# The first batch's transpose: through HBM, or by six copies within SBUF from column-tiled products

## The chip, the cores and the metric

The kernel runs on one core of a Trainium2 chip. The metric is device time in microseconds for one launch; a run of the kernel before takes 618.25 us (median of three). Engines are named as in the profile: PE (TensorE), DVE (VectorE), ACT (ScalarE), POOL (GpSimd) and SP, whose queue issues most of the DMAs.

## The reference, cut to what matters

```python
# x: (8, 3008, 256); w_gate, w_val: (256, 1536); w_out: (1536, 256)
X = np.fft.fft(x, axis=1)          # over the 3008 positions of each batch
X = np.fft.fft(X, axis=2)          # over the 256 channels
y = X.real.reshape(8 * 3008, 256)
g = y @ w_gate
gelu = 0.5 * g * (1 + erf(g / sqrt(2)))
out = (gelu * (y @ w_val)) @ w_out
```

The real part of a two-dimensional Fourier transform is followed by a gated feed-forward block.

## The kernel before, in words

The transform over 3008 = 64 x 47 positions is done in two stages of matmuls. The transform over the channels is folded into the weights: `gen_w` multiplies the cast weights `wb` by a cosine and sine table `CW` and makes three bf16 weight tiles, `WE` (even part), `WOP` (odd part) and `WOM`, which is `WOP` times `col_m` (0 for the first channel, -2 for the others): added to a sum that already holds the `WOP` product, it turns the sign of the odd part.

For each batch:

- `load_x` brings three pieces of x into `xins`; `fold_x` forms sums and differences of channel c and 256 - c into `xf` (batch 0 on DVE, later batches on POOL); `singles` copies the two channels that have no partner.
- Stage one, `a_step(b, k)`: for two of the 24 slots `jj`, one matmul each with weights `G[:, jj, :]` (128 x 128, a table made on the chip by `phase_g`, `sin_g`, `turn_g`) and 256 moving columns `xf[jj]`. The products are copied from PSUM to the tile `S1`.
- The turn: `z_write` stores `S1` to a scratch tensor `z` in HBM, and `z_read` loads it back into `Ap` with other rows on the partitions. In batch 0 there are six writes of four slots each, and after all of them six reads: three thirds, each in two halves of 16 of the 32 groups. Each third lands on every fourth partition of `Ap`; the partitions that no third reaches stay at the zeros that two POOL memsets put there.
- Stage two, `b_steps(b, eo, q)`: for each of 32 groups, a matmul of `Ap` with a table of 47 or 48 columns (`TP`, `TQ`, or `T0P`, `T0Q` for group 0), for the even and the odd part; for batch 0 another 32 with a single weight column. `evac_rest` and `evac_top` copy the results into `Y`.
- The feed-forward block runs in 36 units per batch (three column chunks of `Y` times twelve slices of 128 features): value and gate matmuls with `WE`, `WOP`, `WOM`, Gelu on ACT, products on DVE and POOL into `h`, then the second layer with `Wo_sb`.

The order on each engine is the program's order: the wrapper `_InOrder` keeps every instruction where it is written. Before the first unit the program issues, in this order, tables for stage one, folds, stage one and z writes of batch 0, a few warming matmuls (`warm`), the z reads, loads of the next weights and of batch 1, the tables `CW` and `TP`, `TQ`, `T0P`, `T0Q`, the first quarter `gen_w(0, ...)` of the weights, and stage two of batch 0 in two halves: groups 0 to 15 of the even and the odd part need only the first half of the z reads, groups 16 to 31 need the second. Units 0 to 7 of batch 0 also generate the other weights (`extra`), and from unit 4 on batch 1's stages are woven in.

`CW` has two halves for the 256 channels, each with its phase tile (`phase_c`), its reduction (`reduce_c`) and its sine (`sin_c`).

Of the kernel before, what the change touches and what calls it, by code (L numbers as in the profile page):

```python
# [37 lines left out]
def kernel(  # L38
# [27 lines left out]
    NJ = 48  # L66
# [46 lines left out]
    col_c = [const_pool.tile([128, 1], FP32, name=f"col_c{i}") for i in range(2)]  # L113
# [7 lines left out]
    rowt = work.tile([128, 4 * N2 + 2 * NJ + 2 * NG], FP32, tag="osb", bufs=2, name="rowt")  # L121
    quat = work.tile([128, 4 * N2 + 2 * NJ + 2 * NG], FP32, tag="osb", bufs=2, name="quat")
# [139 lines left out]
    def quats():  # L262
        for o, b0 in ((0, 0.25), (2 * N2, 0.0)):
            vec.tensor_scalar(
                _sub(quat, [[1, 2 * N2]], o), _sub(cols, [[0, 2 * N2]], 1),
                0.25, b0, op0=ALU.mult, op1=ALU.add)

    TO = 4 * N2
    iota(_sub(rowt, [[2 * N2, 2], [1, 2 * N2]], 0), [[0, 2], [1, 2 * N2]], 0, 0)
# [88 lines left out]
    def sin_t(ph, red):  # L358
        s = lambda t, o, n: _sub(t, [[1, n]], o)
        act.activation(TP[:, :], s(red, 0, 2 * N2), AF.Sin, scale=col_w)  # L360
        act.activation(TQ[:, :], s(red, 2 * N2, 2 * N2), AF.Sin, scale=col_w)
        act.activation(s(ph, 0, 2 * NJ), s(red, 4 * N2, 2 * NJ), AF.Sin, scale=col_w)
        act.activation(_sub(TB, [[1, 2 * NG]], 0), s(red, TG, 2 * NG), AF.Sin, scale=col_w)
        for i, t in enumerate((T0P, T0Q)):
            vec.tensor_scalar(
                t[:, :MID], s(ph, i * NJ, MID), cols[:, 3:4], None, op0=ALU.mult)
            vec.tensor_scalar(
# [4 lines left out]
    def cols_c():  # L372
        for t in range(NCH):
            pool.tensor_scalar(col_c[t], col_p, 128.0 * t, 1.0 / C, op0=ALU.add, op1=ALU.mult)

    def phase_c(t):
        both = red2_tile()
        redc.append(both)
        for q, (o, n) in enumerate(((0, 129), (129, 127))):
            pool.tensor_scalar(both[:, o : o + n], rowc[:, o : o + n], col_c[t], 0.25 * (q + 1),  # L380
                               op0=ALU.mult, op1=ALU.add)

    def reduce_c():
        for both in redc:
            reduce_phase(both[:, :C], both[:, C : 2 * C])
        vec.tensor_scalar(col_m, col_p, 1.0, -2.0, op0=ALU.is_ge, op1=ALU.mult)

    def sin_c():
        for t in range(NCH):
            act.activation(  # L390
                _sub(CW, [[1, C]], t * C), redc[t][:, C : 2 * C], AF.Sin, scale=-TWO_PI)
# [13 lines left out]
    def gen_w(f0, i, eo, bank, o=0, n=512):  # L405
# [7 lines left out]
        if eo == 0:  # L413
            on_half(ps, act.activation(WE[:, i, fs], out, AF.Copy))
        else:
            on_half(ps, act.activation(WOP[:, i, fs], out, AF.Copy))
            on_half(ps, vec.tensor_scalar(
                WOM[:, i, fs], out, col_m, None, op0=ALU.mult))
# [627 lines left out]
```

## Time and profile before

| | |
|---|---|
| runs | 618.25 us median of 3 (618.23 to 620.0) |
| profiled execution | 617.78 us, its span 616.0 us |
| PE busy | 600.3 us (97% of the span) |
| DVE busy | 568.8 us (92%) |
| ACT busy | 487.9 us (79%) |
| POOL busy | 503.8 us (82%) |
| first stage-one matmul | 9.1 us from the span's start |
| first matmul of unit 0 | 26.98 us |

Times in the profile count from the first instruction of the span; the rest of the execution's time lies around the span. Busy time is an average over stages with different limits. Matmuls overlap in the records, so the distance between starts says more than the duration of one. The chain of waits goes back from the last instruction to what released each step. The granted TensorE clock reads full in all stretches.

### The profile page before, as it was taken

The page shows a single profiled execution, that of the slowest core. Times are in us where ns is not written, and L with a number is a line of the kernel's source. Part 1 is how long each engine was busy: PE and PEld are TensorE (multiplying, and loading weights), DVE is VectorE, ACT ScalarE, POOL GpSimd, SP SyncE. Part 2 cuts the span into 40 slices and gives each one's busy share as a digit, 9 for nine tenths or more (in the row PEclk, how much of TensorE's full clock was granted, in tenths as well). Part 3 has the DMA queues.
Part 4 walks back from the last instruction along what each step waited for, and adds up shares of the span by engine and source line. Part 5 has one row for each costly group of instructions (what it writes and reads, how often), then busy time and mean ns, then how long its engine had stood idle before and what let it go on. Part 6 is the DMA issues. An engine that isn't in the chain of part 4 may idle for free.

```text
span 616.0 us, 12987 instructions
## 1 busy us (share of the span) xinstructions
PE 600.3 (97%) x4554; PEld 398.7 (65%) x4554; DVE 568.8 (92%) x690; ACT 487.9 (79%) x1009; POOL 503.8 (82%) x521
## 2 busy tenths in 40 slices
PE   3899999999999999999999999999999999999997
PEld 2456666666676666666666666666666666666666
DVE  8688999999999999999999999999999999999992
ACT  8788878977898778877789778887788878767762
POOL 9297999889999899798998899898997755665552
PEclk9999999999999999999999999999999999999999
DMA  8997423662236612663146532375123611211113
GB/s 323 338 296 252 147 61 117 176 199 91 76 121 206 201 44 77 189 227 113 52 131 174 196 95 77 105 222 197 57 67 97 193 49 45 61 50 53 37 51 86
DMA packets 65474, 82.35 MB, mean 134 GB/s; under 512 B 8218, under 2 KB 58906, under 8 KB 62498
## 3 DMA queue, kind: packets, MB, share of 16 engines
q1 hardware_dynamic: 63698, 80.62, 41.7%
q0 software_dynamic: 1552, 0.79, 0.9%
q8 instruction: 35, 0.57, 0.4%
q14 instruction: 29, 0.24, 0.1%
q10 hardware_dynamic: 160, 0.13, 0.1%
HBM read 45.05 MB, written 37.25 MB: 134 GB/s over the span
## 4 chain that ended last, share of the span: by engine, by line
PE 92%; DVE 3%; ACT 2%; DMA 1%; SPq 1%; issue 0%; ACTq 0%; DVEq 0%
PE ps_o L25 38%; PE ps_g L25 28%; PE ps_v L25 20%; PE ps_d L25 6%; DVE xf L25 1%; DMA Ap<-z 1%; DVE dv L25 1%; ACT glp L25 1%; SPq L25 1%; DVE ev L25 0%; DVE h L25 0%; ACT glm L25 0%; ACT S L25 0%; DMA out_dram<-osb 0%; ACT WE L25 0%
## 5 line engine op out<-in xcount | busy, mean ns | idle before, releaser
L25 POOL TENSOR_TENSOR h<-glm,dv 128x1024 bf16<-128x1024 bf16 (+1 forms) x138 | 291.2, 2112 | 82.2 <-DVE dv L25 62.2
L25 PE MATMUL ps_o<-Wo_sb,h 128*128 128x256 bf16 x2124 | 284.2, 272 | 0.0
L25 PEld LDWEIGHTS <-h 128*128 128x128 bf16 x2208 | 211.0, 98 | 58.3 <-issue 0.9
L25 DVE SCALAR_TENSOR_TENSOR ev<-nq,WN,ps_v 128x512 f32<-128x512 bf16 (+1 forms) x276 | 202.1, 733 | 23.0 <-PE ps_v L25 14.7
L25 ACT ACTIVATE glp<-ps_g 128x512 bf16<-128x512 f32 (+1 forms) x288 | 169.9, 590 | 37.0 <-PE ps_g L25 25.3
L25 ACT ACTIVATE glm<-ps_g 128x512 bf16<-128x512 f32 (+1 forms) x241 | 142.2, 590 | 57.4 <-PE ps_g L25 44.5
L25 DVE TENSOR_TENSOR h<-glp,ps_v 128x1024 bf16<-128x1024 bf16 (+2 forms) x150 | 172.9, 1153 | 5.4 <-ACT glp L25 3.7
L25 DVE SCALAR_TENSOR_TENSOR dv<-ev,ps_v 128x1024 f32<-128x1024 f32 (+1 forms) x138 | 164.8, 1194 | 0.0
L25 POOL TENSOR_TENSOR xf<-xin 128x254 bf16<-128x254 f32 x168 | 118.5, 728 | 0.8 <-PE ps_g L25 0.8
L25 PE MATMUL ps_v<-Y,WE 128*128 128x512 bf16 (+1 forms) x288 | 108.0, 375 | 0.0
L25 PE MATMUL ps_v<-Y,WOP 128*128 128x512 bf16 (+1 forms) x288 | 107.7, 374 | 0.1
L25 PE MATMUL ps_g<-Y,WOP 128*128 128x512 bf16 (+1 forms) x288 | 107.6, 374 | 0.0
L25 PE MATMUL ps_g<-Y,WE 128*128 128x512 bf16 (+1 forms) x288 | 107.6, 374 | 0.0
L25 PE MATMUL ps_g<-Y,WOM 128*128 128x512 bf16 (+1 forms) x241 | 90.3, 375 | 0.1
L25 PEld LDWEIGHTS <-WOP 128*128 128x128 bf16 x576 | 55.5, 97 | 49.3 <-ACT WOP L25 0.4
L25 PEld LDWEIGHTS <-WE 128*128 128x128 bf16 x576 | 56.0, 97 | 27.5 <-issue 2.0
L25 ACT ACTIVATE osb<-ps_o 128x512 f32<-128x512 f32 x92 | 54.2, 589 | 13.4 <-PE ps_o L25 12.6
L25 POOL TENSOR_TENSOR go<-go,ge 128x480 f32<-128x480 f32 (+1 forms) x47 | 58.2, 1238 | 7.0 <-DVE go L25 6.5
L25 PEld LDWEIGHTS <-Ap 128*128 128x128 bf16 (+1 forms) x561 | 39.6, 95 | 33.2 <-issue 1.4
L25 ACT ACTIVATE S<-ps_d 128x512 bf16<-128x512 f32 x82 | 48.9, 596 | 0.2 <-PE ps_d L25 0.2
L25 PEld LDWEIGHTS <-G 128*128 128x128 bf16 x213 | 21.8, 103 | 32.5 <-issue 11.0
L25 DVE SCALAR_TENSOR_TENSOR go<-nq,WN,ps_g 128x480 f32<-128x480 bf16 (+1 forms) x47 | 34.3, 729 | 2.6 <-ACT glp L25 1.9
(132 smaller groups left out, 377.1 us busy)
## 6 DMA issues: line engine op xcount, KB each, us to landing
out_dram<-osb SPq DMA_DIRECT2D x358, 64.0 KB
xin<-in_x_dram SPq DMA_DIRECT2D x16, 1024.0 KB
Ap<-z SPq DMA_DIRECT2D x21, 512.0 KB
xin<-in_x_dram SPq DMA_DIRECT2D x8, 896.0 KB
z<-S SPq DMA_DIRECT2D x7, 768.0 KB
z<-S SPq DMA_DIRECT2D x7, 512.0 KB
z<-S SPq DMA_DIRECT2D x13, 256.0 KB
nq<-nrow SPq DMA_DIRECT2D x8, 376.2 KB
```

The costliest lines, as they stand in the source:

```text
L25: return lambda *a, **k: self._tc.keep_in_program_order(call(*a, **k))
```

## The change

Six things are changed, all of them before or around the first units of batch 0.

1. Stage one of batch 0 is done by `a_group(J)`, J = 0 to 5, each for four slots `jj`. For every slot there are four matmuls with 32 of the 128 weight columns each; the outputs of the four slots go to four different ranges of 32 partitions of one PSUM tile. The twelve evacuations are all on ACT.
2. One DMA per group copies `S1` (128 partitions of 2 KB) directly to 16 partitions of `Ap` (every fourth, from `J % 2 * 64 + J // 2`), 16 KB into each. The z writes and z reads of batch 0 are gone. Every group of stage two now reads data of all six copies.
3. `CW`'s second half is formed on ACT from the first by copies with signs +1 and -1, instead of by a phase and sine of its own; the remaining phase is made on ACT, not POOL.
4. The tables `TP` and `TQ` take half as many phases (each is written twice from the same phases); `quats` and the products for `T0P` and `T0Q` move from DVE to POOL; `cols_t` moves ahead of the second fold; the third fold is done in two halves.
5. `WOM` is formed on DVE from `WOP` in SBUF (`turn_w`), not from PSUM; for the first quarter of the weights this comes after unit 0's first-layer matmuls. The first `WE` quarter is evacuated by DVE, not ACT.
6. Order: the tables and the Gelu table load come before `gen_w(0, ...)`; the warming matmuls are 6, not 5 and 16; stage two runs all even groups, then all odd ones, then the single columns, and then the evacuations.

```diff
     def quats():
-        for o, b0 in ((0, 0.25), (2 * N2, 0.0)):
-            vec.tensor_scalar(
+        for o, b0 in ((0, 0.25), (N2, 0.0)):
+            pool.tensor_scalar(
...
     def sin_t(ph, red):
-        act.activation(TP[:, :], s(red, 0, 2 * N2), AF.Sin, scale=col_w)
-        act.activation(TQ[:, :], s(red, 2 * N2, 2 * N2), AF.Sin, scale=col_w)
-        act.activation(s(ph, 0, 2 * NJ), s(red, 4 * N2, 2 * NJ), AF.Sin, scale=col_w)
+        act.activation(s(ph, 0, 2 * NJ), s(red, TO, 2 * NJ), AF.Sin, scale=col_w)
+        for i, t in enumerate((TP, TQ)):
+            act.activation(
+                _sub(t, [[N2, 2], [1, N2]], 0), _sub(red, [[0, 2], [1, N2]], i * N2), AF.Sin, scale=col_w)
...
     def sin_c():
-        for t in range(NCH):
-            act.activation(
-                _sub(CW, [[1, C]], t * C), redc[t][:, C : 2 * C], AF.Sin, scale=-TWO_PI)
+        act.activation(_sub(CW, [[1, C]], 0), redc[0][:, C : 2 * C], AF.Sin, scale=-TWO_PI)
+        for o, sign in ((0, 1.0), (1, -1.0)):
+            act.activation(_sub(CW, [[2, 128]], C + o), _sub(CW, [[2, 128]], o), AF.Copy, scale=sign)
...
         if eo == 0:
-            on_half(ps, act.activation(WE[:, i, fs], out, AF.Copy))
+            on_half(ps, act.activation(WE[:, i, fs], out, AF.Copy) if f0 else
+                    vec.tensor_copy(WE[:, i, fs], out))
         else:
             on_half(ps, act.activation(WOP[:, i, fs], out, AF.Copy))
-            on_half(ps, vec.tensor_scalar(
-                WOM[:, i, fs], out, col_m, None, op0=ALU.mult))
+            if f0:
+                turn_w(f0, i)
+
+    def turn_w(f0, i):
+        vec.tensor_scalar(
+            WOM[:, i, f0 : f0 + 512], WOP[:, i, f0 : f0 + 512], col_m, None, op0=ALU.mult)
...
+    def a_group(J):
+        if "S1" not in st[0]:
+            st[0]["S1"] = S1_tile()
+        S1 = st[0]["S1"]
+        if J % 4 < 2:
+            ps, log = ps_v(), []
+            banks = [(ps[:, h, :], log) for h in range(2)]
+        else:
+            banks = [(f(), []) for f in ((ps_g, ps_g) if J % 4 == 2 else (ps_o, ps_d))]
+        for gq in range(4):
+            for jl in range(4):
+                jj = 4 * J + jl
+                ps, log = banks[gq // 2]
+                apart(log, gq // 2, pe.matmul(
+                    _sub(ps, [[1, C]], gq % 2 * C, 32 * jl, 32),
+                    _sub(G, [[32, 4], [4, 8]], jj * 128 + gq), _sub(xf, [[1, C]], jj * C),
+                    start=True, stop=True))
+        for h in range(2):
+            dst = _sub(S1, [[1, 2 * C]], (4 * J + 2 * h) * C)
+            ps, log = banks[h]
+            apart(log, h, act.activation(dst, ps, AF.Copy))
+        p_step = Ap[:, :, :].ap[0][0]
+        sync.dma_start(
+            out=ap_replace(
+                Ap[:, :, :], ap=[[4 * p_step, 16], [1, NG * C]],
+                offset=Ap[:, :, :].offset + (J % 2 * 64 + J // 2) * p_step),
+            in_=_sub(S1, [[1, 4 * C]], 4 * J * C))
...
+    phase_c()
     turn_g()
     for i in range(3):
-        fold_x(0, i, vec, single=False)
+        for a0, n in ((0, 8),) if i < 2 else ((0, 4), (4, 4)):
+            fold_x(0, i, vec, a0, n, single=False)
         if i == 0:
             singles(0)
+            pool.memset(Ap[:, :16, :].bitcast(FP32), 0.0)
+            cols_t()
+            quats()
             singles(1)
-            pool.memset(Ap[:, :16, :].bitcast(FP32), 0.0)
+            pool.memset(Ap[:, 16:, :].bitcast(FP32), 0.0)
             singles(2)
-            pool.memset(Ap[:, 16:, :].bitcast(FP32), 0.0)
-            for t in range(NCH):
-                phase_c(t)
-        elif i == 2:
-            cols_t()
-        for k in range(4 * i, 4 * i + 4):
-            a_step(0, k)
-            if k % 2:
-                z_write(0, 2 * k - 2, 4)
-    warm(5)
-    for third, half in ((0, 0), (1, 0), (0, 1), (2, 0), (1, 1), (2, 1)):
-        z_read(0, third, 16 * half, 16)
+        for J in range(2 * i, 2 * i + 2):
+            a_group(J)
+    reduce_c()
+    pt = phase_t()
+    warm(6)
...
-    reduce_c()
+    sin_c()
+    sin_t(*pt)
+    act.activation(col_f[:, :], col_p[:, :], AF.Gelu)
     cast_w(0, eng=vec)
-    quats()
-    pt = phase_t()
-    sin_c()
+    vec.tensor_scalar(col_m, col_p, 1.0, -2.0, op0=ALU.is_ge, op1=ALU.mult)
     for i in (1, 0):
         gen_w(0, i, 0, ps_g)
         gen_w(0, i, 1, ps_vh)
-    sin_t(*pt)
-    act.activation(col_f[:, :], col_p[:, :], AF.Gelu)
-    warm(16)
-    later_evacs = []
-    for half in range(2):
...
+    parts = [[b_steps(0, eo, q) for q in range(4)] for eo in range(2)]
+    for part in parts:
+        for q in (1, 0, 2, 3) if part is parts[1] else (2, 1, 3, 0):
+            for s in part[q][0][:8]:
+                s()
+    for q in (1, 0, 2, 3):
+        for s in parts[1][q][0][8:]:
+            s()
+    for eo, part in ((0, 3), (0, 2), (1, 3)):
+        for q in (2, 1, 3, 0):
+            parts[eo][q][part]()
+    later_evacs = [parts[1][q][2] for q in (2, 3, 1, 0)]
+    for i in (1, 0):
+        later_evacs.append(lambda i=i: turn_w(0, i))
```

## The prediction

> **What bounds the kernel now.** I read the page first, then the busy time by stage, then the chain of waits through the first 28 us. The page's chain says TensorE nearly everywhere:
>
> ```profile
> PE 92%; DVE 3%; ACT 2%; DMA 1%; SPq 1%; issue 0%; ACTq 0%; DVEq 0%
> ```
>
> The stretches say where that is not so. Columns: stretch, length, busy us and instructions of PE, PEld, DVE, ACT, POOL, then granted clock, DMA share, GB/s:
>
> ```profile
> 16.60:20.40 3.80, 3.33 (x16) 1.36 (x15) 3.66 (x11) 2.66 (x7) 0.00 (x0) 1.00 0.94 268
> 20.40:25.60 5.20, 4.11 (x65) 2.56 (x64) 3.09 (x14) 3.72 (x11) 0.00 (x0) 1.00 0.98 330
> 27.00:40.00 13.00, 12.58 (x63) 5.73 (x62) 9.68 (x18) 11.25 (x23) 12.04 (x19) 1.00 1.13 346
> 100.00:600.00 500.00, 499.98 (x3749) 334.90 (x3748) 477.29 (x545) 402.50 (x825) 415.80 (x386) 1.00 0.39 118
> ```
>
> From 27 us on TensorE does not stop, and the change touches nothing after batch 0's weights (u = 7). So it can only move the moment at which the units begin; what it gains there is kept to the end. The chain of waits up to that moment:
>
> ```profile
> 11.15 2.35 DVE xf L25 x2
> ...
> 13.55 0.61 PE ps_g L25 x2
> 14.16 0.43 PE ps_v L25 x2
> ...
> 15.47 0.61 ACT S L25
> 16.10 0.36 SPq L25
> ...
> 19.73 5.54 DMA Ap<-z
> 25.27 0.32 issue
> 25.58 0.36 PE ps_v L25 x8
> 25.94 0.20 PE ps_g L25 x8
> 26.15 1.20 PE ps_v L25 x33
> 27.35 0.56 PE ps_g L25 x2
> ```
>
> Read downwards: the folds end at 13.5, the last stage-one product leaves PSUM at 16.1, then SP issues the last z write and six z reads, and the last of them is released at 25.27. Half of batch 0's stage two (48 matmuls) still follows, and unit 0's first odd gate matmul runs at 27.55. From 16.1 to 25.3 the chain has nothing but the way through HBM; the 16 warming matmuls at 19.5 are filler. That 9.2 us is what the change attacks. I carry one mark through: **the odd gate matmul of unit 0, 27.55 us**.
>
> **The folds and GpSimd.** The three small `cols` operations move ahead of the second fold (0.17 + 0.15 + 0.14 = 0.45 us), and the third fold in halves pays two more starts (about 0.1): DVE's folds end near 14.1 instead of 13.5. GpSimd matters more. In before's timeline:
>
> ```profile
> 6.70 1.17 POOL L25 TENSOR_SCALAR col_c<-col_p 128x1 f32<-128x1 f32 x1
> 7.82 2.38 POOL L25 CAST xf<-xin 128x16 bf16<-128x16 f32 x2
> 10.10 1.81 POOL L25 MEMSET Ap<- 128x2048 f32 x1
> ```
>
> A one-column operation takes 1.17 us here because GpSimd operations that read SBUF end just after the DVE fold beside them (the folds take 1.15 each); memsets are not held. Laid out for the new order: first singles to 7.9, first memset to 9.7, the two `quats`, now on GpSimd and after `cols`, each held by a half of the second fold, to 10.7 and 11.8, second singles 12.4, second memset 14.2, third singles about 14.8. Two consequences: groups 2 and 3 start at 12.4, groups 4 and 5 at 14.8; and the first copy, which waits for both memsets of Ap, cannot be issued before 14.2, although its data are ready at 12. On SP everything behind it (five copies, then the next weights) waits too.
>
> **Stage one.** 24 matmuls of 256 columns become 96 whose outputs are 32 partitions. A 256-column matmul with its load takes 0.215 us here (0.43 per pair in the chain). No row shows column groups side by side. Bounds: four together cost what one does, 0.215 per round, 24 rounds = 5.2 us, as now; or each costs it alone, 20.6 us. I take 0.27 per round, near the lower end, since only the weight loads (mean 0.10 us each, partly hidden) come on top: 1.1 us a group, the last group done near 17.0. The Trainium skill (TensorE: Matmul & The Clock Gate, Part 3) says that column tiles at different 32-partition outputs run concurrently and gives 2.38 times for three; no trace here shows it.
>
> **ScalarE.** The two phase copies come ahead of `turn_g` (2 x 0.25, as eight of 64 columns take 2.02), so evacuations start at 11.0, not 10.16, and all twelve are its own (pitch 0.48 from 10.16, 10.74, 11.21). It catches up at group 2 and ends with group 5 near 17.75. Then CW 0.42, two half-turned copies 0.55, four table sines at 0.26 pitch, table load 1.28, one Gelu: 21.2. Before, the same load ended at 22.8. `WOP` follows to 22.2 and the Y evacuations behind it; DVE has `WE` by 21.4. All of that lies beside the copies if they land after about 21; if they land sooner, this chain is what is late next.
>
> **The copies.** Removed: six z writes (1.5 MB in 512 B pieces) and six z reads, 12 SP issues of 0.36 and 0.57 us. Added: six copies of 256 KB each. First data 0.8 us after issue (a store issued at 560.79 has its first packet at 561.61): 15.1. Nothing is queued ahead, because the first loads have drained by 12.9. The rate is the open price. No row copies SBUF to SBUF. These stretches bound it:
>
> ```profile
> 3.00:9.00 6.00, 0.00 (x0) 0.00 (x0) 5.83 (x10) 5.01 (x12) 5.94 (x18) 1.00 0.98 407
> 18.50:23.50 5.00, 5.00 (x44) 2.52 (x43) 3.51 (x11) 4.47 (x10) 0.00 (x0) 1.00 0.95 300
> 561.60:562.00 0.40, 0.40 (x6) 0.37 (x4) 0.40 (x1) 0.25 (x1) 0.40 (x1) 1.00 0.63 161
> ```
>
> Loads over all partitions run at 407 GB/s (0.64 us per 256 KB), the z reads into every fourth partition of Ap at about 300 (0.87), one 64 KB store out of 32 neighbouring partitions at 161 (1.6). I take 0.87: same tile, same partition step, same bytes per transfer. Six: 15.1 + 5.2 = 20.3; the last copy, issued at 17.8, is not later than that. The z reads' last packets are near 24.8 and the release at 25.27, so 0.45 more, and 0.3 until the matmul: stage two starts at 21.05.
>
> **Stage two and the sum.** All 99 matmuls now follow the last copy, against 48 before: 48 took 1.40 us (25.58 to 26.98), 99 take 2.9, giving 24.0. The first odd gate matmul needs DVE's odd evacuations of two blocks, one of which has three pieces (0.33, 0.33, 0.25, 0.17): 0.95 us after the last matmul, where before it was 0.57. Mark: 24.95, against 27.55: 2.6 us earlier. `WOM` formed from SBUF lets PSUM go earlier; TensorE now waits 0.4 us in all for "DVE WOM", but unit 0's `turn_w` is queued ahead of the first product, so I count nothing. The next weights are issued near 18.4 instead of 20.4 and land by about 22.5 for GpSimd's cast (1.03 each), under stage two; without that cover TensorE would wait for gen_w microsecond for microsecond. Sum on the profiled execution: span 616.0 - 2.6 = 613.4, plus 1.8 outside the span (617.78 - 616.0) = 615.2. The median, 618.25, is 0.5 above that execution: **615.7 us**.
>
> **Rivals.**
> *The copies run at half width.* Each copy writes 16 partitions lying in one half of the tile (0 to 60 or 64 to 124), and the store row shows what a narrow set of partitions does: 161 against 407. For: that row. Against: it is a small transfer with its start in it, and neighbouring copies alternate halves. The mark is 19.7 plus six copy times, so each tenth of a microsecond per copy costs 0.6, and the gain is gone at 1.3 us per copy. Between 1.0 and 1.6 the time is 616.4 to 620.0, middle 618.2. The Trainium skill (SBUF — State Buffer, Door 1: The DMA port swizzle) states that partitions 0 to 63 reach only 8 of 16 ports, about 218 GB/s; by it a copy takes an estimated 1.2 us and the kernel 617.6. The store row agrees in direction; no write of this kind is in the trace.
> *The copies are no bound.* At 0.64 us each the last lands at 20.1, and gen_w, WE and WOP hold stage two: mark near 24.4, 615.0; with a quicker stage one, down to 614.3.
> *Column groups run one after another.* Then 96 matmuls cost 0.215 each until the array speeds up (512 columns take 0.42 us at 15.2 and 0.23 at 19.5), later 0.11 to 0.16: if that comes at 12.5, stage one ends between 21 and 25, with 7.1 us from there to the mark. No gain at an end of 20.5, slower by over 0.3% from 22.3; at 23.2 it gives 621.0. For it: nothing in the trace overlaps such matmuls. Against: in the code the four weights and outputs of a round lie in different quarters of 32. The Trainium skill (TensorEngine Tiling (Array Packing), Restrictions and Gotchas) says that column tiling excludes fast weight loads, which speaks for the slow end; untested here.
>
> **Chances.** Forecast, gain 1.85 to 3.1: 0.40. Copies no bound: 0.17. Half width: 0.28, of which 0.02 slower by over 1.85 us. One after another: 0.12, of which 0.09 is. Other: 0.03, mostly within. One measurement tells about 0.3%, 1.85 us, from no change: faster 0.57, same 0.31, slower 0.12. Range 614.2 to 618.7: it takes in both ends of the fast cases and the half-width case up to 1.4 us per copy.
>
> **What would show it.** Right: the first copy issued near 14.2 behind the second memset, copies released about 0.9 us apart, stage two from 21, unit 0's odd gate matmul near 25. Half width: copies 1.2 us or more apart. Serial columns: matmul starts 0.2 us apart within a round and stage one ending past 20. Wrong altogether: a gap on TensorE between 25 and 40 us, or any difference after that.

## The result, and the profile after

The changed kernel takes 620.08 us (median of 20 runs, 618.8 to 620.83) against 617.37 us for the kernel before in the same sittings (20 runs, 616.84 to 620.0): ratio 1.0040, 95% interval 1.0033 to 1.0047. It is slower by 0.4%, where 615.7 was forecast. Its profiled execution took 618.8 us, with a span of 616.8. The 618.25 us from which the forecast started were the median of three runs of the kernel before; its 20 runs put it at 617.37, 0.4 below its profiled execution.

First the page's chain shares of the kernel after. TensorE falls from 92% to 85% of the chain, and DMA rises from 1% to 4%. Only 1% is the copies (6.66 us); the rest lies in later batches' z reads and stores, so this line does not yet say where the time went:

```profile
PE 85%; ACT 4%; DMA 4%; SPq 2%; POOL 2%; issue 1%; DVE 1%; ACTq 0%; POOLq 0%; DVEq 0%
```

The stretches of the kernel after, with the same columns as those of before:

```profile
17.00:22.00 5.00, 3.14 (x12) 1.09 (x10) 1.38 (x2) 4.16 (x11) 1.32 (x4) 1.00 1.06 230
20.40:25.60 5.20, 1.76 (x59) 1.79 (x60) 1.17 (x7) 1.85 (x6) 0.65 (x1) 0.92 1.07 338
24.00:30.00 6.00, 5.95 (x109) 4.35 (x107) 3.86 (x15) 3.55 (x11) 4.37 (x5) 0.72 1.05 408
27.00:40.00 13.00, 12.87 (x70) 6.02 (x69) 10.45 (x24) 11.77 (x24) 12.52 (x22) 0.95 1.16 335
```

In 17 to 22, where the copies and toward the end the first of the next weights move, the DMA engines are fully busy (share 1.06) and yet carry 230 GB/s. In 24 to 30 the granted TensorE clock is 0.72 in the mean (0.50 from 24.82 to 28.23); in the kernel before it was 1.00 in every stretch shown. The chain of waits of the kernel after, early part:

```profile
7.71 1.71 POOL Ap L25
9.42 1.54 POOL quat L25 x2
...
11.39 0.69 POOL xf L25
...
12.12 0.65 PE ps_g L25 x8
...
12.79 3.65 ACT S L25 x8
16.45 6.66 DMA Ap<-S
23.11 0.73 issue
23.84 0.36 PE ps_v L25 x8
...
26.83 1.15 PE ps_v L25 x17
27.98 0.59 PE ps_g L25 x2
```

The evacuations end at 16.45 on the chain, and then comes one piece of 6.66 us: the copies. The way through HBM had been a piece of 5.54 us from 19.73. So this piece starts 3.3 us sooner (the first copy was issued at 13.80, the first z read at 16.63), but it ends only 2.2 us sooner (23.11 against 25.27), and now all 99 matmuls of stage two stand behind them instead of 48. The mark, unit 0's first odd gate matmul, is at 28.18 instead of 27.55.

The units can be compared one by one by the start of their first Gelu on ScalarE (`glp<-ps_g`). Times of before, and what three executions add to them: the profiled one of the kernel after, another of the same kernel (first experiment), and one of it with two hidden VectorE operations more (last experiment):

| unit | before, us | after | after again | after, two VectorE operations more |
|---|---|---|---|---|
| 0 | 27.95 | +0.73 | +1.11 | +1.69 |
| 4 | 34.84 | +0.44 | +1.21 | +2.21 |
| 10 | 46.94 | -0.03 | +0.75 | +1.74 |
| 100 | 227.37 | +0.14 | +0.82 | +1.90 |
| 200 | 428.16 | +0.33 | +1.00 | +2.08 |
| 287 | 600.30 | +0.65 | +1.31 | +2.00 |

Three things are to be read off it. The front loses 0.7 to 1.7 us at unit 0, and the profiled execution is the best of the three. It is also the fastest of the kernel's 20 runs, 1.3 us below their median, while that of the kernel before lies 0.4 us above its median; so the two profiled executions differ by 1.0 us (618.8 - 617.78) and the medians by 2.7. Some of the loss, 0.5 us, is given back between units 4 and 10. And some is lost late, after unit 100.

### The profile page after: what moved, and what is told of

Same layout as the page of the kernel before. It is cut to its first block, busy times and chain, and to the rows that moved or that the text cites. A ratio compares the mean times of both kernels' runs of the same rounds, so it can differ in the third digit from the quotient of the medians.

```text
span 616.8 us, 13035 instructions
## 1 busy us (share of the span) xinstructions
PE 595.6 (97%) x4553; PEld 398.7 (65%) x4611; DVE 565.3 (92%) x684; ACT 488.6 (79%) x1012; POOL 503.7 (82%) x522
## 4 chain that ended last, share of the span: by engine, by line
PE 85%; ACT 4%; DMA 4%; SPq 2%; POOL 2%; issue 1%; DVE 1%; ACTq 0%; POOLq 0%; DVEq 0%
PE ps_o L25 35%; PE ps_g L25 26%; PE ps_v L25 19%; PE ps_d L25 6%; SPq L831 2%; ACT S L25 2%; DMA Ap<-z 2%; DMA Ap<-S 1%; ACT osb L25 1%; DMA out_dram<-osb 1%; ACT glm L25 1%; ACT glp L25 0%; POOL prow L25 0%; POOL quat L25 0%; POOL xf L25 0%
## 5 line engine op out<-in xcount | busy, mean ns | idle before, releaser
L25 POOL TENSOR_TENSOR h<-glm,dv 128x1024 bf16<-128x1024 bf16 (+1 forms) x138 | 290.9, 2110 | 83.8 <-DVE dv L25 65.3
L25 PE MATMUL ps_o<-Wo_sb,h 128*128 128x256 bf16 x2124 | 284.2, 273 | 1.0
L25 PEld LDWEIGHTS <-h 128*128 128x128 bf16 x2208 | 211.0, 98 | 58.3 <-issue 0.9
L25 DVE SCALAR_TENSOR_TENSOR ev<-nq,WN,ps_v 128x512 f32<-128x512 bf16 (+1 forms) x276 | 202.0, 733 | 23.1 <-PE ps_v L25 14.7
L25 ACT ACTIVATE glp<-ps_g 128x512 bf16<-128x512 f32 (+1 forms) x288 | 169.8, 590 | 38.1 <-PE ps_v L25 18.6
L25 ACT ACTIVATE glm<-ps_g 128x512 bf16<-128x512 f32 (+1 forms) x241 | 142.2, 590 | 56.1 <-PE ps_g L25 43.8
L25 DVE TENSOR_TENSOR h<-glp,ps_v 128x1024 bf16<-128x1024 bf16 (+2 forms) x150 | 172.9, 1153 | 5.0 <-ACT glp L25 3.9
L25 DVE SCALAR_TENSOR_TENSOR dv<-ev,ps_v 128x1024 f32<-128x1024 f32 (+1 forms) x138 | 164.7, 1194 | 0.0
L25 POOL TENSOR_TENSOR xf<-xin 128x254 bf16<-128x254 f32 x168 | 118.5, 727 | 0.4 <-PE ps_v L25 0.4
L25 PE MATMUL ps_v<-Y,WOP 128*128 128x512 bf16 (+1 forms) x288 | 107.8, 374 | 0.1
L25 PE MATMUL ps_v<-Y,WE 128*128 128x512 bf16 (+1 forms) x286 | 107.6, 376 | 0.1
L25 PE MATMUL ps_g<-Y,WE 128*128 128x512 bf16 (+1 forms) x266 | 99.6, 375 | 0.0
L25 PE MATMUL ps_g<-Y,WOP 128*128 128x512 bf16 (+1 forms) x257 | 96.1, 374 | 0.8
L25 PE MATMUL ps_g<-Y,WOM 128*128 128x512 bf16 (+1 forms) x241 | 90.4, 375 | 0.2
L25 PEld LDWEIGHTS <-WOP 128*128 128x128 bf16 x576 | 55.6, 97 | 49.3 <-DVE Y L25 0.5
L25 PEld LDWEIGHTS <-WE 128*128 128x128 bf16 x576 | 56.1, 97 | 27.9 <-issue 2.5
L25 ACT ACTIVATE osb<-ps_o 128x512 f32<-128x512 f32 x92 | 54.2, 589 | 13.4 <-PE ps_o L25 12.9
L25 POOL TENSOR_TENSOR go<-go,ge 128x480 f32<-128x480 f32 (+1 forms) x47 | 58.0, 1234 | 7.5 <-DVE go L25 7.1
L25 PEld LDWEIGHTS <-Ap 128*128 128x128 bf16 (+1 forms) x561 | 40.2, 97 | 36.1 <-issue 4.6
L25 ACT ACTIVATE S<-ps_d 128x512 bf16<-128x512 f32 x82 | 48.9, 596 | 0.2 <-PE ps_d L25 0.2
L25 PEld LDWEIGHTS <-G 128*128 128x128 bf16 (+1 forms) x270 | 21.0, 113 | 26.2 <-ACT red L25 3.7
L25 DVE SCALAR_TENSOR_TENSOR go<-nq,WN,ps_g 128x480 f32<-128x480 bf16 (+1 forms) x47 | 34.2, 729 | 2.7 <-ACT glp L25 2.2
```

Of the source, the lines that this page charges most:

```text
L25: return lambda *a, **k: self._tc.keep_in_program_order(call(*a, **k))
```

## The experiments

### Is it the copies' rate, their issue, or the clock?

The changed kernel once more:

> The changed kernel again, for a second profile. Theory A (the six copies move at half rate because each writes 16 partitions of one half of the tile, and while TensorE waits for them its clock falls to half for one or two stretches): again 1.25 us per copy or more, a wait of TensorE of 3.5 us or more before stage two, stage two at 36 ns per matmul instead of 29, 619 to 621 us. Rival D (the difference of 2.5 us has another place, after 40 us): the first odd gate matmul of unit 0 stands where it stood in the first profile, 28.2, and the rest is lost later.

Measured 620.35 us (3 runs, ratio 1.0042, 1.0026 to 1.0058); stage two from 24.26, mark 28.59, granted clock 0.72 again in 24 to 30. The late copies and the fall of the clock are no accident of one execution.

With warming matmuls in the gap:

```diff
+    warm(14)
     parts = [[b_steps(0, eo, q) for q in range(4)] for eo in range(2)]
```

> Fourteen warming matmuls (3.2 us) put between gen_w of the first quarter and stage two, the rest as changed. Theory A: stage two starts at the same 23.8, but its 99 matmuls take 2.9 us instead of 3.56 and the first units run at full clock; 1 to 2 us faster than the changed kernel, 618 to 619. If the clock has no part in it: the same as the changed kernel, 620.

Measured 619.50 us (6 runs, ratio 1.0029, 1.0017 to 1.0041). The stretch 24 to 30 of this kernel:

```profile
24.00:30.00 6.00, 5.56 (x111) 3.57 (x112) 4.34 (x15) 3.72 (x11) 4.00 (x5) 1.00 1.06 410
```

The clock stays at 1.00, and 99 matmuls take 2.68 us instead of 3.56. From the start of stage two to the mark it is 3.40 us (24.27 to 27.67) instead of 4.34. The fall of the clock is thus worth about 0.9 us; between the medians it is 0.6 (0.85 against the three runs of the repeat), less than the 1 to 2 us expected. The other 1.9 us stay, so the clock is an effect of the gap and not the main cause.

The same number of bytes, issues and sources, but 128 destination partitions instead of 16 (stage two then gets other data):

```diff
-            out=ap_replace(
-                Ap[:, :, :], ap=[[4 * p_step, 16], [1, NG * C]],
-                offset=Ap[:, :, :].offset + (J % 2 * 64 + J // 2) * p_step),
+            out=_sub(Ap, [[1, 4 * C]], (16 + 4 * J) % NG * C),
```

> Each copy writes the same 256 KB to 128 partitions (four groups of Ap each) instead of 16, so stage two gets other data than the reference's; sources, sizes, order and the wait on the second memset stay. Theory A (width): 2 KB packets near 85 ns, 0.65 us per copy, the copies all landed near 20, stage two at 20.5, mark near 25, 614 to 615. Rival B (a copy within SBUF is slow as such): packets stay near 155 ns and the time at 620. Rival C (SP's issue of 0.81 us each sets the pace): packets fast, but the last one released only about 1.5 us earlier than now, 617 to 618.

Measured 615.48 us (6 runs, ratio 0.9968, 0.9956 to 0.9980), mark 24.09, no fall of the clock. SyncE's issues were where they had been (13.81, 4.69 us in all). So neither the issues nor SBUF-to-SBUF copies as such are slow: it is the 16 destination partitions. With this rate the change would have come near the forecast time.

The HBM turn put back into the new order:

```diff
-        for J in range(2 * i, 2 * i + 2):
-            a_group(J)
+        for k in range(4 * i, 4 * i + 4):
+            a_step(0, k)
+            if k % 2:
+                z_write(0, 2 * k - 2, 4)
+    for third, half in ((0, 0), (1, 0), (0, 1), (2, 0), (1, 1), (2, 1)):
+        z_read(0, third, 16 * half, 16)
```

> Only the turn undone: stage one by full-width products, z writes and z reads of the kernel before, inside the changed order of everything else. Theory A: the z reads end at about 25, and all 99 matmuls of stage two follow them, against 48 before: mark at 29 to 29.5, 619 to 620 and so no better than the copies. Rival E (the new order of tables and weights is what costs, not the copies): slower than the changed kernel's 620 by nothing, and slower than before by the full 2.5 us although the reads end at 25.3 as before.

Measured 620.69 us (4 runs, ratio 1.0054, 1.0037 to 1.0071), stage two from 24.63, mark 29.20. The time is 0.7 us above the expected range. The copies are not slower than the HBM turn in the same place. What the new order gives up, against the kernel before, is the half of stage two that ran under the second half of the transfers, and the clock. This kernel shows no late loss: unit 10 is at +1.15 and unit 287 at +1.16.

### What in the 16 partitions is slow?

The mean time of a packet can be had from the DMA line of a stretch (packets, MB, share of 16 engines): share x 16 x length / packets. Kernel after, 17 to 22 us:

```profile
q1 hardware_dynamic: 633, 1.15, 106.1%
```

That is 1.061 x 16 x 5 = 85 us of packet time for 561 packets of 2 KB and 72 of a few bytes: 0.15 us each. The wide copies, 15 to 19 us:

```profile
q1 hardware_dynamic: 648, 1.20, 81.7%
```

52.3 us for 585 packets of 2 KB: 0.089 us each. Where the partitions lie was then varied in two runs. Step 7 instead of 4, so that the 16 rows of a copy go from 0 to 110:

```diff
-                Ap[:, :, :], ap=[[4 * p_step, 16], [1, NG * C]],
-                offset=Ap[:, :, :].offset + (J % 2 * 64 + J // 2) * p_step),
+                Ap[:, :, :], ap=[[7 * p_step, 16], [1, NG * C]],
+                offset=Ap[:, :, :].offset + J * p_step),
```

> Row i of copy J lands in partition 7i + J of Ap instead of 4i + J/2 + 64 (J mod 2); the per-partition tables and the later batches' z reads (six of 16 partitions instead of three of 32) follow the new order, so the result is the reference's. Each copy still writes 16 partitions, but from 0 to 110. Theory A in the form of the Trainium skill (SBUF, the port swizzle: partitions are tied to 16 ports; these 16 partitions reach 14 or 15 of them, those of the changed kernel 8): packets of 2 KB near 84 to 100 ns instead of 155, copies paced by their issue (0.81 us each) as in the wide copies, stage two from 20 to 21.4, mark 24.1 to 25.0, time 615.5 to 616.3. Rival W (16 destination partitions are too few, wherever they lie): packets stay near 155 ns, stage two near 24, time near 620.

> As the kernel with step 7, but row i of copy J lands in partition 8i + J: spread over the whole tile, 0 to 125, yet by the port swizzle of the Trainium skill only 8 of the 16 ports. Theory A as ports: packets stay near 155 ns, stage two near 24, mark near 28, time near 620. Theory A as halves of the tile (a copy is slow because its 16 partitions lie below or above 64): as fast as step 7, time 615.5 to 616.3. Rival W: as slow as step 7, near 620.

Measured 620.52 us for step 7 (4 runs, ratio 1.0048, 1.0031 to 1.0065) and 622.85 us for step 8 (4 runs, 1.0096, 1.0078 to 1.0114). Stretch 17 to 22 of step 7 and of step 8:

```profile
q1 hardware_dynamic: 686, 1.27, 97.8%
```

```profile
q1 hardware_dynamic: 569, 1.04, 106.6%
```

Packets of 2 KB take 0.125 us with step 7 and 0.166 with step 8. "Halves of the tile" falls: step 8 covers the whole tile and is the slowest. With step 7 a third of the packets in this stretch (212 of 620) took 80 to 90 ns, in the profiled kernel after 1 of 561; but in its repeat, where one issue took 1.96 us and the copies met less, it was 125 of 524, with 0.136 us a packet. So step 7 is a small gain at most, the time did not come down, and from this pair alone rival W could not be dismissed. Step 8 is also slower than any of the three theories had it (near 620), but 1.8 us of that is a wait at unit 21 for a z read of batch 1 (`PE ps_d L25 <- DMA Ap<-z: 1.8, 1, 1.8` in its waits).

Each copy in two of 8 rows, so that no two rows of a transfer are 32 partitions apart:

```diff
-        sync.dma_start(
-            out=ap_replace(
-                Ap[:, :, :], ap=[[4 * p_step, 16], [1, NG * C]],
-                offset=Ap[:, :, :].offset + (J % 2 * 64 + J // 2) * p_step),
-            in_=_sub(S1, [[1, 4 * C]], 4 * J * C))
+        for k in range(2):
+            sync.dma_start(
+                out=ap_replace(
+                    Ap[:, :, :], ap=[[4 * p_step, 8], [1, NG * C]],
+                    offset=Ap[:, :, :].offset + (J % 2 * 64 + 32 * k + J // 2) * p_step),
+                in_=_sub(S1, [[1, 4 * C]], 4 * J * C, 64 * k, 64))
```

> Each copy of the changed kernel in two of 8 destination rows (64 source partitions each), same partitions of Ap: rows 4i for i below 8 first, then the 8 rows 32 partitions further on, so no two rows of a transfer are 32 partitions apart. Theory A as ports (two rows 32 partitions apart share a port, by the Trainium skill, SBUF, the port swizzle, and two DMA engines then take turns at it): 2 KB packets near 84 to 95 ns where one transfer is under way, though fewer of them run at once, so the rate may stay near 200 GB/s. Rival W (a row of one partition cannot be written faster, or the reads are the slow side): packets stay at 145 to 155 ns or more and the rate falls. Stage two between 23.5 and 27, depending on how many engines a transfer of 8 rows keeps busy; time 619.5 to 623.

Measured 623.55 us (2 runs, ratio 1.0098, 1.0080 to 1.0117), stage two from 27.40, mark 32.10. Stretch 16 to 23:

```profile
q1 hardware_dynamic: 618, 1.12, 48.5%
```

Half of the DMA engines are idle (the Trainium skill, DMA: Bandwidth & Descriptors, section "Why a DMA increments its semaphore by 16 and not by 1", has a transfer use the largest number up to 16 that divides the rows on both its sides, here 8; the 48.5% agrees). But the packets are quick: 0.098 us in the mean, and 437 of 548 at 80 to 90 ns. One partition's row can be written at the full pace of its engine, so rival W falls as it was put. That half the engines rest would explain why this kernel is slower; its twelve issues also keep SyncE until 22.8 us.

That left the number of engines open as a cause, so four of the six copies got 16 rows without such pairs, partitions 32 + 4i, still on 16 engines:

```diff
+        step, p0 = ((2, 0), (2, 96), (4, 32), (4, 33), (4, 34), (4, 35))[J]
         sync.dma_start(
             out=ap_replace(
-                Ap[:, :, :], ap=[[4 * p_step, 16], [1, NG * C]],
-                offset=Ap[:, :, :].offset + (J % 2 * 64 + J // 2) * p_step),
+                Ap[:, :, :], ap=[[step * p_step, 16], [1, NG * C]],
+                offset=Ap[:, :, :].offset + p0 * p_step),
```

> The changed kernel with another order of Ap's partitions: copies 2 to 5 go to partitions 32 + 4i + (J - 2), that is 32 to 95, where no two of the 16 rows are 32 partitions apart on the same side of 64; copies 0 and 1 go to 2i and 96 + 2i, where rows still pair up. The tables, and the z reads of the later batches (six of 16 rows), follow; the result is the reference's. Ports: packets of copies 2 to 5 near 84 to 95 ns, those of 0 and 1 near 150; copies 2 to 5 then follow SyncE's issues (0.81 each), the last lands near 20.3, stage two from 20.5 to 21.5 instead of 23.84, mark 24.3 to 25.2, and with the late loss and a wait for batch 1's z reads of 0 to 1 us the time is 616.0 to 617.5. Number of engines (the 8-row halves had quick packets only because half the engines were at work): packets stay near 150 ns, stage two near 23.8, time near 620.

Measured 618.90 us (6 runs, ratio 1.0025, 1.0014 to 1.0036). Stretch 19 to 21, in which such copies follow each other:

```profile
DMA packets 355, 0.66 MB, mean 329 GB/s; under 512 B 34, under 2 KB 34, under 8 KB 355
...
q1 hardware_dynamic: 355, 0.66, 101.0%
```

0.10 us a packet and 329 GB/s with all 16 engines at work, against 0.15 and 230. Of the copies, only the destination partitions differ. So the price of a copy goes with such pairs: rows i and i + 8 of a copy lie 32 partitions apart on the same side of 64, and where both are written at the same time a packet takes 0.15 us instead of 0.10. That two such rows share a port is what the Trainium skill states (SBUF — State Buffer, section "Door 1: The DMA port swizzle": 128 partitions on 16 ports, and 32 further on is the same port). The runs agree with its table in the order of the kernels: 8 ports 0.14 to 0.17 us a packet, 14 or 15 ports 0.125, one row to a port 0.10. The estimate from it in the prediction, 1.2 us a copy, was nearly right.

Two things stay open: why step 8, with 8 ports like the kernel after, is slower than it, and why the z reads of the kernel before, whose 32 rows hold the same pairs, are not slowed as much. In 18.5 to 23.5 us their queue moved 1.49 MB at a share of 94.6%, which is 0.10 us for 2 KB, mostly in packets of 8 KB. Whether the longer packets or the source in HBM makes the difference, no run shows.

The time of this kernel was missed (616.0 to 617.5 expected): stage two began at 23.70. The new tables cost GpSimd more, so the second memset ended at 14.38 instead of 13.78; one of the six issues on SyncE took 2.17 us where the others took 0.54 to 0.67; and 1.72 us lay between the last piece of copying in the chain (to 21.98) and the first matmul, where the profiled kernel after had 0.73:

```profile
18.74 3.24 DMA Ap<-S
21.98 1.72 issue
23.70 0.48 PE ps_v L25 x8
```

The last two also turn up in other kernels, or do not, and what decides it is open.

### When can the copies start, and from which queue?

Both memsets of Ap right behind the first singles on GpSimd:

```diff
             pool.memset(Ap[:, :16, :].bitcast(FP32), 0.0)
+            pool.memset(Ap[:, 16:, :].bitcast(FP32), 0.0)
             cols_t()
+            singles(1)
+            singles(2)
             quats()
-            singles(1)
-            pool.memset(Ap[:, 16:, :].bitcast(FP32), 0.0)
-            singles(2)
```

> Both memsets of Ap come right behind the first singles on GpSimd, the second and third singles and the two quats behind them; all else as in the changed kernel. Theory A (each copy moves at half width; the six of them are a serial stretch that begins when the second memset ends): the first copy is issued near 12.0 instead of 13.80 and the six still take 1.25 to 1.4 us each, so stage two starts near 22.0 instead of 23.84, TensorE idles 1.5 us less and its clock does not fall, mark near 26.3 instead of 28.18, time near 618.2. If the copies were limited by when stage one delivers (last evacuation 16.9) and not by their own rate, the start moves by less than 0.5 us and the time stays near 620.

Measured 617.36 us (10 runs, ratio 0.9997, 0.9988 to 1.0006). Chain of waits of this kernel:

```profile
10.88 4.79 ACT S L25 x11
15.67 5.57 DMA Ap<-S
21.25 0.73 issue
21.98 0.36 PE ps_v L25 x8
...
25.34 0.04 issue
25.38 0.38 PE ps_g L25
```

The first copy is issued at 11.88, stage two starts at 21.98 as expected, and the mark is 25.38: 2.2 us before that of the kernel before, and yet the median, though better than the 618.2 expected, is no better than its. The profiled execution (616.74) is the fastest of the ten; in 8 of the nine others the clock over the whole run was 0.996 or 0.997 instead of 1.0, so in them the clock had fallen too. In the chain the copies still are one piece of 5.57 us. The earlier memset on GpSimd brought stage two forward by 1.9 us (21.98 against 23.84), since the copies are a serial stretch that begins behind it.

The odd copies from ScalarE, so that both halves of Ap can be written at once:

```diff
-        sync.dma_start(
+        (sync, act)[J % 2].dma_start(
```

> The kernel with both memsets early, and the odd copies issued by ScalarE instead of SyncE, so that a copy into the lower and one into the upper half of Ap can be under way together. Theory A (a half can take only half the rate): packets near 84 to 110 ns while two copies overlap, 300 GB/s or more, all six landed by about 20 instead of 21.9; but ScalarE pays three issues of about 0.8 us, its evacuations and tables end 2.4 us later (Gelu table from 20.9 instead of 18.51), so the units start where they did or later: mark 25.4 to 26.5, time 617.0 to 618.5. Rival W: packets stay near 150 ns, mark near 27, time near 619.

Measured 620.06 us (8 runs, ratio 1.0042, 1.0032 to 1.0052), mark 27.70; 617.0 to 618.5 was expected. Timeline of ScalarE and then of TensorE in this kernel:

```profile
12.81 0.62 ACTq L25 DMA_DIRECT2D Ap<-S  x1
13.48 1.08 ACT L25 ACTIVATE S<-ps_g 128x512 bf16<-128x512 f32 x2 [0.75 <-PE ps_d L25]
```

```profile
20.35 1.06 PE L25 MATMUL ps_v<-wb,CW 128*128 128x512 bf16 x2
...
24.30 0.36 PE L25 MATMUL ps_v<-TP,Ap 128*128 128x47 bf16 x8 [1.18 <-ACT WOP L25]
```

In 13 to 18 us, where only copies are under way, 248 of 484 packets took 80 to 90 ns, against 178 of 563 in the kernel with early memsets alone. So two copies into different halves disturb each other somewhat less, but fewer packets went through in the same time. And every issue holds up the evacuations behind it on ScalarE: `CW` is formed later, the table is loaded at 20.91 instead of 18.51, and stage two now waits for `WOP`. The wait has moved to another engine. TensorE, which had waited 2.32 us for `CW`, also ran the matmuls of `gen_w` at a granted clock of 0.50 (20.0 to 23.3 us): a pair took 1.06 us in the record above, 0.60 in the kernel after.

### Where does the late loss come from?

Between units 100 and 287 the kernel after loses 0.5 us, always at units 184 to 186, 216, 218 and 258; 0.13 comes back at 237. ScalarE's timeline near unit 184, kernel before and then kernel after:

```profile
395.57 0.57 ACT L25 ACTIVATE glm<-ps_g 128x480 bf16<-128x480 f32 x1
396.23 0.58 ACT L25 ACTIVATE glp<-ps_g 128x481 bf16<-128x481 f32 x1
```

```profile
395.71 0.57 ACT L25 ACTIVATE glm<-ps_g 128x480 bf16<-128x480 f32 x1
396.65 0.58 ACT L25 ACTIVATE glp<-ps_g 128x481 bf16<-128x481 f32 x1 [0.37 <-PE ps_d L25]
```

The Gelu starts 0.37 us later than it could; the releaser named is a later matmul on which it does not depend. Two ideas were tried: TensorE's longer program, and ScalarE's.

```diff
-    warm(16)
+    ps = ps_d()
+    for _ in range(88):
+        pe.matmul(ps[:, :96], G[:, 0, :], _sub(G, [[1, 96]], 0), start=True, stop=True)
```

> The kernel before with its 16 warming matmuls of 512 columns replaced by 88 of 96 columns (8448 columns instead of 8192, at the same place, 72 more matmuls and 72 more weight loads, 144 instructions, the number by which the changed kernel's TensorE program is longer). Theory L (the 0.5 us that the changed kernel loses between 396 and 549 us comes of the longer instruction program, at places where code has to be brought in): unit 0's odd gate matmul stays near 27.55, and the same jumps of 0.13 to 0.23 us appear at units 184 to 186, 216, 218 and 258 to 260, 0.4 to 0.5 us in all. Rival: the late loss belongs to the 32-row products or the data layout, and the later units keep the pace of the kernel before within 0.1 us.

Measured 618.71 us in one run. From unit 22 to the end the pace is that of the kernel before within 0.03 us: theory L falls. The 1.0 us that this execution lost is a wait at unit 21 (`PE ps_d L25 <- DMA Ap<-z: 1.0, 1, 1.0` in its waits) for batch 1's last z read, which comes just in time or a little late: the wait is nothing in the profiled execution of before, 0.4 with the warming matmuls, 0.7 with step 7, 1.8 with step 8 and 1.1 in the last two kernels below. Part of the spread from run to run may be this wait; one profile for a kernel cannot show it.

```diff
-    act.activation(col_f[:, :], col_p[:, :], AF.Gelu)
+    for _ in range(3):
+        act.activation(col_f[:, :], col_p[:, :], AF.Gelu)
```

> The kernel before with two more one-column Gelu activations behind the one that loads ScalarE's table (0.2 us each, while everything waits for the z reads). Theory P (the late loss of 0.5 us follows the place of ScalarE's instructions in its program: the changed kernel and all its kin that show the jumps have 2 more instructions there than the kernel before, the two kernels without jumps have as many as it): the jumps at units 184 to 186, 216, 218, 237 and 258 to 260 appear, in sum 0.4 to 0.5 us later at the last unit than at unit 100. Rival: they come of the 32-row products or of GpSimd's, VectorE's or SyncE's shorter programs, and none appears here.

Measured 616.93 us in one run. ScalarE's timeline of this kernel:

```profile
394.45 0.57 ACT L25 ACTIVATE glm<-ps_g 128x480 bf16<-128x480 f32 x1
395.39 0.57 ACT L25 ACTIVATE glp<-ps_g 128x481 bf16<-128x481 f32 x1 [0.37 <-PE ps_d L25]
```

The same wait at the same unit: two more instructions on ScalarE, 370 us earlier, bring it into the kernel before. The jumps at 216, 218 and 258 did not come, so theory P was half right as put. The traces tell them apart by VectorE: all nine profiles with the jumps at 216, 218 and 258 have 939 records on it, waits for semaphores included; the others have 940, 941 or 946 (the counts in the expectation below are two higher). So, on the changed kernel:

```diff
-    vec.tensor_scalar(col_m, col_p, 1.0, -2.0, op0=ALU.is_ge, op1=ALU.mult)
+    for _ in range(3):
+        vec.tensor_scalar(col_m, col_p, 1.0, -2.0, op0=ALU.is_ge, op1=ALU.mult)
```

> The changed kernel with two more one-column operations on VectorE behind the cast of the first weights (0.15 us each, in its idle time), 943 instructions instead of 941, as in the kernel with the HBM turn and the one with the sign copies moved; ScalarE's program is as in the changed kernel. Theory P for both engines (a late stall follows the place of an engine's instructions): the jumps at 216, 218 and 258 go, those at 184 to 186 and 237 stay. Rival: the jumps at 216, 218 and 258 stay, and hang on something else that the changed kernel and its kin share.

Measured 620.14 us in one run: the jumps at 216, 218 and 258 are gone, those at 184 to 186 and 237 stay. From unit 200 to 287 this kernel gains 0.08 on the kernel before where the kernel after loses 0.32. The late loss thus goes with how many instructions ScalarE and VectorE had before, not with what the change computes. All 17 profiles fit that: the ten with 1467 records on ScalarE jump at 184 to 186, the five with 1465 do not. The copies in 8-row halves, with one record more on each engine (1468 and 940), jump at units 133 to 136 instead, and the kernel with three issues on ScalarE (1473) at 80 and 183. Why a certain place costs 0.1 to 0.4 us (the fetching of code would be the obvious idea) no run shows.

### A version that is faster

Both memsets early, warming matmuls in the gap, and the two sign copies of CW on VectorE, which takes two instructions from ScalarE and gives two to VectorE:

```diff
-        for o, sign in ((0, 1.0), (1, -1.0)):
-            act.activation(_sub(CW, [[2, 128]], C + o), _sub(CW, [[2, 128]], o), AF.Copy, scale=sign)
...
+    for o, sign in ((0, 1.0), (1, -1.0)):
+        vec.tensor_scalar(_sub(CW, [[2, 128]], C + o), _sub(CW, [[2, 128]], o), sign, None, op0=ALU.mult)
...
+    warm(11)
```

> The kernel with both memsets early, plus eleven warming matmuls ahead of stage two (19.1 to 21.7 in the gap of 2.74 us), and the two sign copies of CW on VectorE instead of ScalarE, which gives ScalarE the program length of the kernel before. From the runs so far: the copies are at half rate still, stage two from 22.0, 99 matmuls in 2.65 us, mark 25.4 against 27.55; no clock fall (worth 0.85 us where it happens); no late loss if theory P holds. Profiled execution near 616.2 (span 614.2), median near 616.3, ratio 0.998; it would be the fastest of the correct kernels and still within 0.3% of the kernel before. Without theory P 616.8.

Measured 616.82 us (11 runs, ratio 0.9991, 0.9982 to 1.0000), 0.5 above what was expected: no late loss (unit 22 to 287 within 0.03 us of before) and the clock at 1.00, but in the profiled execution the copies ended 0.6 later than in the kernel with early memsets alone (stage two from 22.59), and unit 21 waited 1.1 us.

The same without the warming matmuls, with copies 2 to 5 in partitions 32 + 4i:

> The partition order of the kernel just named, with both memsets early and the two sign copies of CW on VectorE. Ports: the first copies run from 12.7 while stage one goes on, the last is issued near 17 and lands near 19; then gen_w (its last product near 19.2) and the WOP evacuations (to 20.5) are as late as the copies: stage two from 19.3 to 20.3, mark 23.2 to 24.0 against 27.55. Off that: up to 1.2 us of waiting for batch 1's z reads at unit 21, 0.2 outside the span, no late loss. Time 614.0 to 615.5, ratio 0.994 to 0.997, the first version that beats the kernel before by more than 0.3%. Number of engines: as the kernel with both memsets early and the sign copies moved, 616.8.

Measured 616.42 us (12 runs, 614.68 to 617.12, ratio 0.9980, 0.9971 to 0.9988). Apart from the wide copies it is the only kernel whose interval lies below 1: 0.94 us better than before, less than the 0.3% expected, and 0.9 above the 615.5 that closed the expected range. Its chain, and its waits at unit 21:

```profile
18.68 1.28 ACT L25
...
20.18 0.98 ACT WOP L25 x2
21.16 0.35 issue
21.51 0.36 PE ps_v L25 x8
```

```profile
PE ps_d L25 <- DMA Ap<-z: 1.1, 1, 1.1
```

The copies are no longer in this part of the chain: stage two, from 21.51, waits for ScalarE's table and `WOP`, as the prediction had named what would be late next. The mark is 24.91, where the prediction had put it (24.95); of these 2.6 us, 1.1 go to the wait for batch 1's z reads.

## Why the prediction was wrong, point by point

**What bounds the kernel, and the mark.** Right in kind: nothing from unit 7 on belongs to the change, and where the mark moved, the units moved with it (e.g. -2.2 at the mark and -1.9 at unit 100 with early memsets). What the mark did not cover was the last half microsecond.

**GpSimd's order.** Right: the second memset gates the copies. It ended at 13.78 (14.2 forecast) and the first issue was at 13.80:

```profile
11.97 1.81 POOL L25 MEMSET Ap<- 128x2048 f32 x1
13.80 4.88 SPq L25 DMA_DIRECT2D Ap<-S  x6
```

**Stage one.** Right, on the good side. The timeline of TensorE in the kernel after:

```profile
8.88 1.90 PE L25 MATMUL ps_v<-xf,G 128*32 128x256 bf16 x32 [3.65 <-DVE cols L25]
12.12 1.05 PE L25 MATMUL ps_g<-xf,G 128*32 128x256 bf16 x16 [1.34 <-POOL xf L25]
...
14.13 1.90 PE L25 MATMUL ps_v<-xf,G 128*32 128x256 bf16 x32
```

32 matmuls in 1.90 us are 0.237 a round of four (0.27 forecast, 0.86 if each had cost 0.215 alone): column tiles do run side by side. The third rival is refuted.

**ScalarE.** Right: evacuations ended at 16.86 (17.75), the one-column Gelu behind the table load at 20.24 (21.2), beside the copies.

**The copies. This is the step that failed:** "I take 0.87: same tile, same partition step, same bytes per transfer". From the first data at 15.07 (15.1 forecast; 1.27 after the issue instead of 0.8, which the earlier issue made up for) to the release at 23.11 it was 8.0 us, where the sum had 5.65 (5.2 and 0.45 for the release): 1.34 us a copy with the release, about 1.27 without the 0.45. The z reads wrote 32 rows from HBM, on both sides of 64; a copy writes 16 on one side, in pairs 32 partitions apart, and with such pairs gone four copies ran at 0.10 us a packet instead of 0.15. Same tile and same step did not make the z reads a measure for it. The 64 KB store out of 32 partitions (161 GB/s, 1.6 us per copy), which the rival took, was the nearer row. The rival of half width was right in its mechanism and, with the 1.3 us at which it let the gain end, nearly in its price. Of the 3.2 us by which the mark was missed (28.18 - 24.95), 2.8 lie before stage two (23.84 - 21.05): 2.4 are the copies, and 0.4 the way from the release to the first matmul, 0.73 instead of 0.3.

**The 99 matmuls at 2.9 us.** They took 3.56, because TensorE had idled for 3.7 us and its clock was at 0.50 from 24.82 on; 2.68 where it did not fall. No rival had that: the price of a longer gap is also paid behind the gap. The Trainium skill (TensorE: Matmul & The Clock Gate, Part 1, "What's actually happening") gives half clock after an idle window of about 3.4 us, and says that this window runs freely and so is not tied to where a gap begins; the trace agrees, with 0.72 to 0.78 granted in 24 to 30 after gaps of 3.7 to 4.8 us and 1.00 after the 2.7 us in the profiled execution with early memsets. But in 8 of that kernel's 9 other runs the mean clock was below 1.0, and with the odd copies from ScalarE the clock fell to 0.50 after a gap of only 2.32 us. So the length of one gap alone does not decide it.

**`WOM` from SBUF, counted at nothing.** It was probably worth some 0.4 us: the kernel before waits (`PE ps_d L25 <- DVE WOM L25: 0.4, 1, 0.4` in its waits between 30 and 42 us, at 35.85), the kernel after has no such wait, and that would be most of the 0.5 us that come back between units 4 and 10 in the table. No run changes this step alone.

**"Any difference after that" would be wrong altogether.** It was there, and it was not the copies' mechanism: 0.5 us late, which goes with the lengths of two engines' programs. And the execution takes 2.0 us outside its span instead of 1.8.

**The sum.** Unit 10 of the profiled execution is level with before (-0.03). From there to unit 287 it loses 0.7 us and outside the span 0.2; these are most of its 1.0 us. The sum took the kernel's median as 0.5 above its profiled execution; it is 1.3 above, and in the two other executions seen unit 10 stands 0.8 and 1.8 us later than in the profiled one. The start of the sum was off as well: 618.25 for the kernel before, whose 20 runs give 617.37. Against that, the forecast was a gain of 2.55 us and the result is a loss of 2.7.

## What to carry to other kernels

Cost a transfer by the partitions it touches, not only by its bytes: before a turn within SBUF replaces one through HBM, write down the 16 or 32 rows and look for pairs that are 32 apart on the same side of 64 (here 0.15 us a packet with them, 0.10 without). When a transfer is made to start earlier, look first at what ran under the old one's tail (here half of stage two, and the warm clock), for it will then stand behind the new one. And a difference of a few tenths of a microsecond far from an edit need not be a mechanism of the edit: shift the programs of the engines by two idle instructions before looking for one.

## What was not expected of the hardware

- Copies with pairs of rows 32 partitions apart took 0.15 us for a 2 KB packet, without such pairs 0.10, into 128 partitions 0.089; step 8, the widest spread, was the slowest at 0.166.
- Four matmuls of 256 columns into four quarters of 32 output partitions took 0.237 us together, where one with 128 took 0.215.
- Two more one-column instructions on ScalarE or VectorE moved stalls of 0.1 to 0.37 us several hundred microseconds later in the program, in both directions.
- One issue of a copy on SyncE took 1.2 to 2.2 us in most of the profiled kernels, the others 0.5 to 0.8; and between the last piece of copying and the matmul that waited for it lay 0.35 us in the two kernels with warming matmuls in the gap, 0.73 or 1.5 to 1.7 in others. Both are open.
